# Another order for the first steps of a chunked state-space scan with a squared-ReLU network

## The chip, the cores and the metric

The kernel runs on one core of one Trainium2 chip. The metric is the device time of one launch in microseconds, the median of three runs.

## The reference

Two stages, float32 in and out. Batch 4, 8 heads, 768 positions, head dimension D = 32, state dimension N = 16, chunks of 32; the network has 256 inputs and 2048 hidden units.

```python
for c in range(24):                                  # chunks of 32 positions
    cum = cumsum(log(clip(a[c], 1e-6, 1)))
    L = exp(cum[i] - cum[j]) * (i >= j)
    y = ((C @ B.T) * L) @ x + (C @ state) * exp(cum)
    state = exp(sum(la)) * state + sum_j B[j] x[j] exp(cum[-1] - cum[j])
h = relu(y.reshape(3072, 256) @ w_in)                # 256 -> 2048
out = (h * h) @ w_out                                # 2048 -> 256
```

## The kernel before, in words

Work is cut into 12 units (`UNITS`): unit k is one batch and 256 positions, all 8 heads; units 0 to 3 are the first 256 positions of the four batches. In a unit two positions (r = 0, 1) share a partition, and two halves (i or u = 0, 1) of 64 partitions each are carried through. A unit gives 256 rows of y, held transposed in a tile `T`, and these rows then go through the network as block a, b, c and so on, in 8 tiles of 256 hidden units each.

Nothing is scheduled by the compiler's order: `ORDER` is a string, and `one` reads it word by word and records one step for each word, on the engine that the step or the word's suffix names (v VectorE or DVE, a ScalarE or ACT, p GpSimd or POOL, s SyncE or SP). Every engine and every DMA queue runs its own steps in this order, and steps of different engines wait for each other by semaphores. So moving a word moves the step in the queue of its engine, and only there. Loads on SP and ACT share eight completion semaphores in turn; a load waits until the one eight loads ahead of it has landed.

The words that the change and the prediction touch, in the sequence of the work:

- `idn:c`: n matmuls of ones on c columns into a free PSUM bank (L476), which compute nothing that is used and keep TensorE (PE) busy.
- `fa1:a`, `fa0:s` load a for units 0 to 3 in two halves (L115); `la` loads a for the other units (L553, "late a"). `ldC0:l:a` loads heads 0 to 3 of C for unit 0 on ACT's queue, `ldC0:h:s` heads 4 to 7 on SP's, `ldB2:s` all of B for unit 2 (L125).
- `gB2`, `gB3`: a memset of one column of that unit's B tile on POOL (L134). A load of that tile issued later must wait for it, and so must every load behind it on SP.
- `ku`, `ef`, `eb`, `ti`, `pi`, `hd`, `mb`, `pk`, `wm`: constants (identity, causal mask, head selectors; L480, L490, L507, L511, L512) and a first ACT instruction, which loads its table (L487). `jz` zeroes one of the three tiles `jt` (L685).
- `sk`: clip and running product of a (L468, L469); `sp`: its transpose by matmul (L452); `su`, `to`, `fq`, `ps`, `iv`: chunk totals, copies and reciprocals of the running product. `sn1`, `p2`, `pq` are the same for the later units.
- `pc`, `pb`, `px`: C times the running product and B into `jt`, x over the running product into `xs` (L158, L168 or L170, L177). `tr`, `trC`, `trB`: `jt` transposed by PE (L195) and copied by `tc` from PSUM into `bct` (L208, L210). From unit 4 on one DMA transpose on SP does both (L186).
- `mt`: scores of a unit, 16 matmuls (L220). Four masks per unit: `mk` by DVE from PSUM (L229), or `sc` copied out by ACT (L234) and `ms` masked from that copy by POOL or DVE (L238).
- `u`: the unit's contribution to the state (L245); `sf` scales it (L343), `ca` applies the state to C, `in` (or `ina`, `inb` in halves) masked scores times xs (all L245). `t0:aa` copies the two halves of y of unit 0 into `T` on ACT, `t0:av` on ACT and DVE (L208, L210); `us` copies the state out.
- `wi`, `wo`: the four tiles each of w_in and w_out, converted to bf16 by POOL's DMA (L139, L143).
- `a0` to `l7`: first layer of block a to l, hidden tile 0 to 7, with ReLU on ACT (L403, L408); `qa0` and so on: the square on DVE (L414); `A0` to `L7`: second layer (L430), and with tile 7 the output copy and its store on SP (L437, L438).
- `fr` gives one PSUM bank back to the steps that follow.

The change lies in the first seven lines of the string; from `a7 qa5 iv:16:32 px2` on the words are the same.

Of the kernel before, what the change touches and what calls it, by code (L numbers as in the profile page):

```python
# [30 lines left out]
def kernel(  # L31
# [16 lines left out]
    ORDER = """
        id13:128 fa1:a la fa0:s ku ef ldx0:h:a eb id6:128 ti id5:128 gB3 pi ldB0:l:a hd ldC0:l:a ldB0:h:s ldC0:h:s
        ldx0:l:a wm jz0:v mb jz1:v ldB1:s id10:128 sk pbh0:a id11:128 pk pbl0:p wi0 sp pc0:v ldC1:s trB0 wi1 su  # L50
        iv1:0:8 trC0 tcC0:0:v tcB0:2:a id5:128 tcC0:1:a ps pb1:a to px0:v jz2:v mt0 id4:128 u0:67 ldx1:s pc1:p fq
        sc0 mk0 id5:128 mk0 ms0:p tr1 tc1:1:v sc0 tc1:0:a sf0 mt1 ldB2:s wo0 ldC2:s ms0:v ldx2:s id3:128 in0 ca0
        iv:8:16 id7:256 px1:p t0:aa id1:128 mk1 a0 a1 mk1 mk1 mk1 u1 ina1 inb1 sn1 us0 sf1 qa0 a3 ldC3:s wi2 fr p2
        wi3 ca1 qa1 wo1 pc2 pb2:a t1:vv us1 iv:32:64 a2 zb0 qa2 zb1 A0 ldB3:s wo2 ldx3:s b3 qb3 b0 pq b2 b1 tr2
        wo3 sb1 qa3 qb0 A1 b5 b4 qb1 qb2 qb5 tc2:1:v qb4 tc2:0:a a5 B0 b6 B1 a7 qa5 iv:16:32 px2 a6 mt2 B3 A2 sc2
        u2 b7 us2 pb3:a pc3 mk2 qa6 px3 mk2 A5 ms2:v mk2 ld4 qb6 sf2 a4 qa7 B5 pc4 A6 A3 ld5 pb4 ina2 inb2 tr4 ca2
        t2:aa tr3 B4 B2 tc3:0:a tc3:1:a u3:45 qb7 ld6 ld7 mt3 qa4 B6 mk3 mk3 mk3 mk3 us3 c4 c5 c0 A4 A7 B7 c6 qc0
        za3 qc4 c1 qc5 qc6 sa3 px4 qc1 pc5 pb5 bk c2 rg4 tr5 C0 mk4 mk4 qc2 c7 qc7 sb0 c3 qc3 d2 d1 C5 za4 afC2 d0
        C1 px5 C4 qd2 zb3 C6 C3 qd0 d3 C2 mk4 mk4 C7 px6 sa4 rg5 qd3 sb3 pc6 zb4 sb4 pb6 D0 d4 qd1 tr6 mk5 za5 zb5
        sa5 sb5 D1 iv:64:96 mk5 d5 qd4 D2 pb7 d6 qd5 d7 qd6 D3 zb2 e0 qd7 mk5 e1 qe0 sb2 D4 mk5 D5 ld8 pc7 e2 qe1  # L60
        D6 e3 qe2 px7 D7 rg6 e4 qe3 za6 sa6 tr7 zb6 mk6 e5 qe4 sb6 e6 qe5 e7 qe6 mk6 E0 E1 E2 E3 ld9 px8 mk6 f0
        qe7 E4 f1 qf0 pc8 E5 pb8 E6 mk6 f2 qf1 f3 qf2 E7 rg7 mk7 F0 f4 qf3 za7 tr8 F1 F2 f5 qf4 f6 qf5 f7 qf6 g0
        qf7 zb7 sa7 sb7 mk7 F3 mk7 F4 pc9 pb9 px9 ld10 g1 qg0 F5 mk7 g2 qg1 F6 g3 qg2 F7 rg8 za8 zb8 sa8 sb8 g4
        qg3 G0 mk8 tr9 g5 qg4 G1 mk8 g6 qg5 G2 g7 qg6 G3 mk8 h0 qg7 G4 pc10 pb10 px10 ld11 h1 qh0 G5 mk8 h2 qh1 G6
        h3 qh2 G7 rg9 za9 zb9 sa9 sb9 h4 qh3 H0 mk9 tr10 h5 qh4 H1 mk9 h6 qh5 H2 h7 qh6 H3 mk9 i0 qh7 H4 pc11 pb11
        px11 i1 qi0 H5 mk9 i2 qi1 H6 i3 qi2 H7 rg10 za10 zb10 sa10 sb10 i4 qi3 I0 mk10 tr11 i5 qi4 I1 mk10 i6 qi5
        I2 i7 qi6 I3 mk10 j0 qi7 I4 j1 qj0 I5 mk10 j2 qj1 I6 j3 qj2 I7 rg11 za11 zb11 sa11 sb11 j4 qj3 J0 mk11 j5
        qj4 J1 mk11 j6 qj5 J2 j7 qj6 J3 mk11 k0 qj7 J4 k1 qk0 J5 mk11 k2 qk1 J6 k3 qk2 J7 rg12 k4 qk3 K0 k5 qk4 K1
        k6 qk5 K2 k7 qk6 K3 l0 qk7 K4 l1 ql0 K5 l2 ql1 K6 l3 ql2 K7 l4 ql3 L0 l5 ql4 L1 l6 ql5 L2 l7 ql6 L3 ql7"""
# [694 lines left out]
```

## Time and profile before

| | |
|---|---|
| three runs | 117.47, 116.82, 117.33 us; median 117.33 us |
| the profiled execution | span 115.2 us from the first to the last instruction; no other time is given for it |
| PE matmuls | 108.6 us busy, 94% of the span, 1674 instructions |
| DVE, ACT, POOL | 84.4, 76.7, 49.5 us busy |
| DMA | 13.47 MB; the queue of SP takes 44.8% of 16 engines' span, the weights' queue 10.9% |

Busy time is counted from the first to the last instruction, issue of DMAs not included. Matmuls overlap: a row of x4 with 0.60 us follows the next row after 0.44 us. PEld is the weight load of TensorE, "DMA share" the mean busy share of the 16 DMA engines (over 1 where packets of two kinds overlap), and an "issue" in a chain is time in which the engine waited for nothing that the profile shows. "DMA to landing" is from the start of the issuing instruction to the last byte's completion. Times in the rows are from the start of the span.

### The profile page before, as it was taken

The page shows a single profiled execution, that of the slowest core. Times are in us where ns is not written, and L with a number is a line of the kernel's source. Part 1 is how long each engine was busy: PE and PEld are TensorE (multiplying, and loading weights), DVE is VectorE, ACT ScalarE, POOL GpSimd, SP SyncE. Part 2 cuts the span into 40 slices and gives each one's busy share as a digit, 9 for nine tenths or more (in the row PEclk, how much of TensorE's full clock was granted, in tenths as well). Part 3 has the DMA queues.
Part 4 walks back from the last instruction along what each step waited for, and adds up shares of the span by engine and source line. Part 5 has one row for each costly group of instructions (what it writes and reads, how often), then busy time and mean ns, then how long its engine had stood idle before and what let it go on. Part 6 is the DMA issues. An engine that isn't in the chain of part 4 may idle for free.

```text
span 115.2 us, 4100 instructions
## 1 busy us (share of the span) xinstructions
PE 108.6 (94%) x1674; PEld 97.4 (85%) x1674; DVE 84.4 (73%) x187; ACT 76.7 (67%) x161; POOL 49.5 (43%) x102
## 2 busy tenths in 40 slices
PE   7978799999999979999999999999999999999990
PEld 7956589988898959989989989989989899899980
DVE  2469989688699969969965989849668488445530
ACT  0665568966598464787486686786777776876840
POOL 7378972067895675548602669038020020000000
PEclk9999999999999999999999999999999999999998
DMA  0999999999979945908818628442041020020202
GB/s 19 203 179 164 193 212 185 211 192 179 185 133 185 308 73 128 173 1 190 153 41 178 130 93 156 100 126 42 0 136 32 0 94 6 1 90 0 95 1 91
DMA packets 47815, 13.47 MB, mean 117 GB/s; under 512 B 44276, under 2 KB 45876, under 8 KB 47796
## 3 DMA queue, kind: packets, MB, share of 16 engines
q1 hardware_dynamic: 43828, 10.64, 44.8%
q0 software_dynamic: 1664, 2.10, 10.9%
q10 hardware_dynamic: 2304, 0.48, 2.0%
q8 instruction: 13, 0.21, 0.8%
q14 instruction: 6, 0.05, 0.2%
HBM read 10.58 MB, written 3.15 MB: 119 GB/s over the span
## 4 chain that ended last, share of the span: by engine, by line
PE 83%; DMA 7%; DVE 2%; issue 1%; POOL 1%; ACTq 1%; ACT 1%; POOLq 0%
PE pp L403 36%; PE pp L430 34%; PE pp L245 7%; DMA bct<-jt 5%; PE pp L220 4%; DMA B_nat<-in_B_dram 3%; PE pp L476 1%; DVE mts L229 1%; PE pp L195 1%; POOL xs L177 1%; PE pp L452 1%; DVE xs L177 1%; ACTq L125 0%; POOL jt L170 0%; ACTq L115 0%
## 5 line engine op out<-in xcount | busy, mean ns | idle before, releaser
L408 ACT ACTIVATE hb<-pp 128x512 bf16<-128x512 f32 x96 | 55.0, 599 | 26.0 <-PE pp L403 24.4
L430 PE MATMUL pp<-w_out_b,h 128*128 128x256 bf16 (+1 forms) x400 | 54.3, 268 | 0.0
L414 DVE TENSOR_TENSOR h<-hb 128x512 bf16<-128x512 bf16 x96 | 46.0, 497 | 11.2 <-ACT hb L408 10.8
L403 PE MATMUL pp<-T,w_in_b 128*128 128x256 bf16 x384 | 54.2, 273 | 0.0
L403 PEld LDWEIGHTS <-w_in_b 128*128 128x128 bf16 x384 | 41.4, 114 | 2.0 <-issue 1.0
L430 PEld LDWEIGHTS <-h 128*128 128x128 bf16 x400 | 37.6, 98 | 4.3 <-issue 0.8
L229 DVE TENSOR_TENSOR mts<-pp,mask 128x512 bf16<-128x512 f32 x45 | 29.6, 678 | 4.1 <-PE pp L220 4.1
L331 POOL TENSOR_TENSOR Sd<-z,Pquad 128x256 bf16<-128x256 f32 x16 | 11.0, 690 | 32.1 <-DVE z L315 25.9
L177 POOL TENSOR_TENSOR xs<-x_nat,Pinv 128x256 bf16<-128x256 f32 (+1 forms) x19 | 14.5, 777 | 6.5 <-DVE Pinv L546 3.7
L158 POOL TENSOR_TENSOR jt<-C_nat,P_sb 128x128 bf16<-128x128 f32 x22 | 9.6, 453 | 1.9 <-DMA C_nat<-in_C_dram 1.3
L476 PE MATMUL pp<-const-bfloat16-1.0 128*128 128x128 bf16 (+1 forms) x70 | 7.4, 281 | 0.8 <-PEq L748 0.8
L476 PEld LDWEIGHTS <-const-bfloat16-1.0 128*128 128x128 bf16 x70 | 6.4, 129 | 1.3 <-issue 1.2
L315 DVE SCALAR_TENSOR_TENSOR z<-z,Ptot,us 128x64 f32<-128x64 f32 x8 | 2.2, 281 | 6.3 <-ACT us L299 5.4
L245 PE MATMUL pp<-mts,xs 64*32 64x128 bf16 x384 | 6.0, 219 | 0.8 <-issue 0.8
L437 ACT COPY osb<-pp 128x512 f32<-128x512 f32 x11 | 6.3, 583 | 0.4 <-PE pp L430 0.4
L220 PE MATMUL pp<-bct 32*64 32x256 bf16 x192 | 5.1, 279 | 1.4 <-DMA bct<-jt 0.7
L170 POOL CAST jt<-B_nat 128x128 bf16<-128x128 f32 x17 | 5.0, 318 | 1.6 <-DVE a_cl L468 1.6
L245 PEld LDWEIGHTS <-xs 64*32 64x32 bf16 x384 | 4.1, 90 | 1.4 <-issue 1.2
L282 ACT CAST T<-pp 128x512 bf16<-128x512 f32 x7 | 4.1, 592 | 0.4 <-PE pp L245 0.2
L245 PE MATMUL pp<-bct,Sd 128*128 128x128 bf16 x40 | 4.2, 219 | 0.0
L208 ACT CAST T<-pp 128x256 bf16<-128x256 f32 x8 | 2.6, 375 | 2.4 <-PE pp L245 2.3
L220 PEld LDWEIGHTS <-bct 32*64 32x64 bf16 x192 | 2.1, 102 | 2.4 <-DMA bct<-jt 0.8
...
## 6 DMA issues: line engine op xcount, KB each, us to landing
...
B_nat<-in_B_dram SPq DMA_DIRECT2D x11, 128.0 KB, 3.8
C_nat<-in_C_dram SPq DMA_DIRECT2D x11, 128.0 KB, 3.8
...
x_nat<-in_x_dram ACTq DMA_DIRECT2D x2, 128.0 KB, 3.6
bct<-jt SPq DMA_TRANSPOSE x8, 2.8
```

The source lines that it names most:

```text
L158: eng.tensor_tensor(out=_fap(jt[k % 3], 128 + 144 * g, [[384, 2], [32, 4], [1, 16]]), in0=_fap(loaded[k]["C"], 128 * g, [[16, 2], [32, 4], ...
L177: eng.tensor_tensor(out=_fap(xs, 256 * r, [[256, 2 // n], [32, 8], [1, 32]]), in0=_fap(loaded[k]["x"], 32 * r, [[32, 2 // n], [64, 8], [1, ...
L220: nc.tensor.matmul(pp[64 * u:64 * u + 64, q, r * 256:r * 256 + 256], bct[32 * q:32 * q + 32, r, 0, u * 64:u * 64 + 64], _fap(bct[32 * q:32 ...
L229: nc.vector.tensor_tensor(out=live[k]["mts"][:, q].rearrange("p r g i -> p (r g i)"), in0=pp[:, q, :], in1=mask, op=ALU.mult)
L245: nc.tensor.matmul(dst, w, v, start=bool(need), stop=False, skip_group_check=True, **({} if pos is None else {"tile_position": pos}))
L331: nc.gpsimd.tensor_tensor(out=_fap(S_d, 0, [[128, 2], [32, 4], [1, 32]]), in0=_fap(z, 0, [[32, 2], [0, 4], [1, 32]]), in1=_fap(Pquad, 4 * ...
L403: nc.tensor.matmul(pp[:, h, i * 256:(i + 1) * 256], _fap(w, g * w.shape[2] + (o // 2) * 512 + 2 * (o % 2) + i, [[4, 128]]), T[blk][:, g].r ...
L408: nc.scalar.activation(out=hb.rearrange("p i t -> p (i t)"), in_=pp[:, h, :], func=AF.Relu)
L414: nc.vector.tensor_tensor(out=h2, in0=hb, in1=hb, op=ALU.mult)
L430: nc.tensor.matmul(dst, h2[:, i, r * 128:(r + 1) * 128], w_out_b[gi][:, 2 * o + i, c0:c1], start=first, stop=(fp == 7 and i == 1), skip_gr ...
L437: nc.scalar.copy(out=osb, in_=pp[:, 6 if blk == 1 else 7, :])
L476: nc.tensor.matmul(pp[:, h, 0:int(cols)], ones_b[:, 0:128], ones_b[:, 0:int(cols)] if dep is None else dep, start=True, stop=True, skip_gr ...
```

## The change

The first seven lines of `ORDER` are written anew; no function changes. On SP, a, C, B and x of unit 0 come before late a; on ACT the loads of unit 0 come in the order a, C, B, x, the heads of x in one load on each queue. The first w_in tile is issued on POOL ahead of the copy of B of unit 0, and the first w_out tile ahead of the masks. The scan of a is recorded ahead of the causal mask. Idle matmuls are 12 of 512 columns instead of 63 of 128 and 7 of 256. The gate on unit 3's B is gone, and one on unit 2's B stands behind unit 1's C, so that unit 2's loads and all behind them on SP wait for it. Unit 0's masks, state, product and `T` follow each other directly, ahead of the transposes of unit 1; the zeroing of the third `jt` comes after them. The second scan moves behind the first tiles of blocks a and b, whose order changes too.

```diff
     ORDER = """
-        id13:128 fa1:a la fa0:s ku ef ldx0:h:a eb id6:128 ti id5:128 gB3 pi ldB0:l:a hd ldC0:l:a ldB0:h:s ldC0:h:s
-        ldx0:l:a wm jz0:v mb jz1:v ldB1:s id10:128 sk pbh0:a id11:128 pk pbl0:p wi0 sp pc0:v ldC1:s trB0 wi1 su
-        iv1:0:8 trC0 tcC0:0:v tcB0:2:a id5:128 tcC0:1:a ps pb1:a to px0:v jz2:v mt0 id4:128 u0:67 ldx1:s pc1:p fq
-        sc0 mk0 id5:128 mk0 ms0:p tr1 tc1:1:v sc0 tc1:0:a sf0 mt1 ldB2:s wo0 ldC2:s ms0:v ldx2:s id3:128 in0 ca0
-        iv:8:16 id7:256 px1:p t0:aa id1:128 mk1 a0 a1 mk1 mk1 mk1 u1 ina1 inb1 sn1 us0 sf1 qa0 a3 ldC3:s wi2 fr p2
-        wi3 ca1 qa1 wo1 pc2 pb2:a t1:vv us1 iv:32:64 a2 zb0 qa2 zb1 A0 ldB3:s wo2 ldx3:s b3 qb3 b0 pq b2 b1 tr2
-        wo3 sb1 qa3 qb0 A1 b5 b4 qb1 qb2 qb5 tc2:1:v qb4 tc2:0:a a5 B0 b6 B1 a7 qa5 iv:16:32 px2 a6 mt2 B3 A2 sc2
+        id3:512 fa1:a fa0:s ef jz0:v ldC0:l:a ldC0:h:s eb id2:512 ldB0:l:a ldB0:h:s hd ti ldx0:l:a ldx0:h:s la ku pi
+        id1:512 sk wm mb jz1:v wi0 ldB1:s ldC1:s sp id1:512 pk id1:512 pc0:v iv1:0:8 trC0 su pbh0:a pbl0:p tcC0:0:v
+        tcC0:1:a trB0 wi1 tcB0:2:a id1:512 px0:v ps to mt0 fr id1:512 u0:67 ldx1:s wo0 fq sc0 mk0 id1:512 mk0 sc0
+        ms0:p sf0 ms0:v pb1:a pc1:p ca0 in0 t0:av jz2:v iv:8:16 tr1 tc1:1:v tc1:0:a id1:512 a0 mt1 gB2 ldB2:s ldC2:s
+        ldx2:s px1:p a1 wi2 wi3 mk1 mk1 mk1 mk1 u1 ina1 inb1 sf1 ca1 wo1 pc2 pb2:a us0 t1:va us1 a2 a3 qa0 qa1 zb0
+        zb1 b0 b1 qa2 qa3 ldC3:s wo2 ldB3:s ldx3:s b2 qb0 qb1 b3 A0 A1 qb2 qb3 wo3 B0 B1 sn1 tr2 sb1 b5 b4 qb5
+        tc2:1:v qb4 tc2:0:a p2 pq iv:32:64 a5 b6 a7 qa5 iv:16:32 px2 a6 mt2 B3 A2 sc2
...
```

More of the change, by code (lines that the diff above doesn't have):

```diff
@@ L54 @@
-        wi3 ca1 qa1 wo1 pc2 pb2:a t1:vv us1 iv:32:64 a2 zb0 qa2 zb1 A0 ldB3:s wo2 ldx3:s b3 qb3 b0 pq b2 b1 tr2
-        wo3 sb1 qa3 qb0 A1 b5 b4 qb1 qb2 qb5 tc2:1:v qb4 tc2:0:a a5 B0 b6 B1 a7 qa5 iv:16:32 px2 a6 mt2 B3 A2 sc2
-        u2 b7 us2 pb3:a pc3 mk2 qa6 px3 mk2 A5 ms2:v mk2 ld4 qb6 sf2 a4 qa7 B5 pc4 A6 A3 ld5 pb4 ina2 inb2 tr4 ca2
-        t2:aa tr3 B4 B2 tc3:0:a tc3:1:a u3:45 qb7 ld6 ld7 mt3 qa4 B6 mk3 mk3 mk3 mk3 us3 c4 c5 c0 A4 A7 B7 c6 qc0
-        za3 qc4 c1 qc5 qc6 sa3 px4 qc1 pc5 pb5 bk c2 rg4 tr5 C0 mk4 mk4 qc2 c7 qc7 sb0 c3 qc3 d2 d1 C5 za4 afC2 d0
@@ L59 @@
[L59 to L68, printed above, removed]
@@ L69 @@
-        k6 qk5 K2 k7 qk6 K3 l0 qk7 K4 l1 ql0 K5 l2 ql1 K6 l3 ql2 K7 l4 ql3 L0 l5 ql4 L1 l6 ql5 L2 l7 ql6 L3 ql7"""
+        id3:512 fa1:a fa0:s ef jz0:v ldC0:l:a ldC0:h:s eb id2:512 ldB0:l:a ldB0:h:s hd ti ldx0:l:a ldx0:h:s la ku pi
+        id1:512 sk wm mb jz1:v wi0 ldB1:s ldC1:s sp id1:512 pk id1:512 pc0:v iv1:0:8 trC0 su pbh0:a pbl0:p tcC0:0:v
+        tcC0:1:a trB0 wi1 tcB0:2:a id1:512 px0:v ps to mt0 fr id1:512 u0:67 ldx1:s wo0 fq sc0 mk0 id1:512 mk0 sc0
+        ms0:p sf0 ms0:v pb1:a pc1:p ca0 in0 t0:av jz2:v iv:8:16 tr1 tc1:1:v tc1:0:a id1:512 a0 mt1 gB2 ldB2:s ldC2:s
@@ new lines @@
+        ldx2:s px1:p a1 wi2 wi3 mk1 mk1 mk1 mk1 u1 ina1 inb1 sf1 ca1 wo1 pc2 pb2:a us0 t1:va us1 a2 a3 qa0 qa1 zb0
+        zb1 b0 b1 qa2 qa3 ldC3:s wo2 ldB3:s ldx3:s b2 qb0 qb1 b3 A0 A1 qb2 qb3 wo3 B0 B1 sn1 tr2 sb1 b5 b4 qb5
+        tc2:1:v qb4 tc2:0:a p2 pq iv:32:64 a5 b6 a7 qa5 iv:16:32 px2 a6 mt2 B3 A2 sc2 u2 b7 us2 pb3:a pc3 mk2 qa6 px3
+        mk2 A5 ms2:v mk2 ld4 qb6 sf2 a4 qa7 B5 pc4 A6 A3 ld5 pb4 ina2 inb2 tr4 ca2 t2:aa tr3 B4 B2 tc3:0:a tc3:1:a
+        u3:45 qb7 ld6 ld7 mt3 qa4 B6 mk3 mk3 mk3 mk3 us3 c4 c5 c0 A4 A7 B7 c6 qc0 za3 qc4 c1 qc5 qc6 sa3 px4 qc1 pc5
@@ new lines @@
+        pb5 bk c2 rg4 tr5 C0 mk4 mk4 qc2 c7 qc7 sb0 c3 qc3 d2 d1 C5 za4 afC2 d0 C1 px5 C4 qd2 zb3 C6 C3 qd0 d3 C2 mk4
+        mk4 C7 px6 sa4 rg5 qd3 sb3 pc6 zb4 sb4 pb6 D0 d4 qd1 tr6 mk5 za5 zb5 sa5 sb5 D1 iv:64:96 mk5 d5 qd4 D2 pb7 d6
+        qd5 d7 qd6 D3 zb2 e0 qd7 mk5 e1 qe0 sb2 D4 mk5 D5 ld8 pc7 e2 qe1 D6 e3 qe2 px7 D7 rg6 e4 qe3 za6 sa6 tr7 zb6
+        mk6 e5 qe4 sb6 e6 qe5 e7 qe6 mk6 E0 E1 E2 E3 ld9 px8 mk6 f0 qe7 E4 f1 qf0 pc8 E5 pb8 E6 mk6 f2 qf1 f3 qf2 E7
+        rg7 mk7 F0 f4 qf3 za7 tr8 F1 F2 f5 qf4 f6 qf5 f7 qf6 g0 qf7 zb7 sa7 sb7 mk7 F3 mk7 F4 pc9 pb9 px9 ld10 g1 qg0
@@ new lines @@
+        F5 mk7 g2 qg1 F6 g3 qg2 F7 rg8 za8 zb8 sa8 sb8 g4 qg3 G0 mk8 tr9 g5 qg4 G1 mk8 g6 qg5 G2 g7 qg6 G3 mk8 h0 qg7
+        G4 pc10 pb10 px10 ld11 h1 qh0 G5 mk8 h2 qh1 G6 h3 qh2 G7 rg9 za9 zb9 sa9 sb9 h4 qh3 H0 mk9 tr10 h5 qh4 H1 mk9
+        h6 qh5 H2 h7 qh6 H3 mk9 i0 qh7 H4 pc11 pb11 px11 i1 qi0 H5 mk9 i2 qi1 H6 i3 qi2 H7 rg10 za10 zb10 sa10 sb10
+        i4 qi3 I0 mk10 tr11 i5 qi4 I1 mk10 i6 qi5 I2 i7 qi6 I3 mk10 j0 qi7 I4 j1 qj0 I5 mk10 j2 qj1 I6 j3 qj2 I7 rg11
+        za11 zb11 sa11 sb11 j4 qj3 J0 mk11 j5 qj4 J1 mk11 j6 qj5 J2 j7 qj6 J3 mk11 k0 qj7 J4 k1 qk0 J5 mk11 k2 qk1 J6
@@ L70 @@
+        k3 qk2 J7 rg12 k4 qk3 K0 k5 qk4 K1 k6 qk5 K2 k7 qk6 K3 l0 qk7 K4 l1 ql0 K5 l2 ql1 K6 l3 ql2 K7 l4 ql3 L0 l5
+        ql4 L1 l6 ql5 L2 l7 ql6 L3 ql7"""
     WIN = [(0, 2), (2, 4), (4, 6), (6, 8)]
```

## The prediction

> **What bounds the kernel now.** I read the page first, then the stretches by time, then the chain of waits, then the timeline of the first 17 us engine by engine, and last the DMA.
>
> ```profile
> span 115.2 us, 4100 instructions
> PE 108.6 (94%) x1674; PEld 97.4 (85%) x1674; DVE 84.4 (73%) x187; ACT 76.7 (67%) x161; POOL 49.5 (43%) x102
> ```
>
> The span is 115.2 us; the median of the three runs, 117.33 us, has 2.1 us around it. The sums below are made in the span, and what they give is taken off 117.33. TensorE (PE) is the bound on average. The stretches, whose columns are length, busy time by engine, clock, DMA share and GB/s, say where it isn't:
>
> ```profile
> 14.45:42.10 27.65, 27.64 (x449) 24.19 (x448) 24.21 (x52) 20.09 (x46) 16.77 (x32) 1.00 1.06 189
> 7.00:8.00 1.00, 0.83 (x19) 0.73 (x19) 0.79 (x3) 0.46 (x3) 0.43 (x1) 1.00 0.68 141
> 10.00:11.00 1.00, 0.81 (x44) 0.61 (x51) 1.00 (x5) 0.00 (x0) 0.81 (x2) 1.00 0.84 134
> 16.00:24.00 8.00, 8.00 (x91) 7.37 (x89) 6.39 (x18) 7.33 (x18) 2.65 (x5) 1.00 1.21 199
> ```
>
> From 14.45 to 42.10 PE is full. The chain of waits (start, length, what) names one wait ahead of that and one behind it:
>
> ```profile
> 13.64 0.80 issue
> 37.51 5.21 DMA bct<-jt
> ```
>
> The timeline has the second wait's end, with the idle time before it in brackets:
>
> ```profile
> 42.76 0.42 PE L220 MATMUL pp<-bct 32*64 32x256 bf16 x16 [0.67 <-DMA bct<-jt]
> ```
>
> So there are two regimes. Before 14.45 the order of small steps sets when PE becomes full. At 42.76 unit 5's scores (L220) wait for a DMA transpose of jt. After that nothing in the trace holds PE up. A gain of g in the front therefore reaches the end only if that transpose comes earlier too: the scores start at the later of (42.09 - g) and (42.72 - d), with d what the transpose gains.
>
> **The front, step by step.** Rows of the timeline are start, length, engine, line, operation and count; the landing row belongs to the two loads above it.
>
> ```profile
> 0.80 0.39 ACTq L115 DMA_DIRECT2D a_nat<-in_a_dram  x1
> 1.61 0.42 SPq L115 DMA_DIRECT2D a_nat<-in_a_dram  x1
> DMA to landing us min/median/max: 1.7/2.4/3.2
> 4.91 0.22 DVE L468 TENSOR_SCALAR a_cl<-a_nat 64x128 f32<-64x128 f32 x1 [1.23 <-DMA a_nat<-in_a_dram]
> 5.16 0.42 DVE L469 TENSOR_TENSOR_SCAN cp<-a_cl,const-float32-0.0 64x128 f32<-64x128 f32 x1
> 0.85 4.75 PE L476 MATMUL pp<-const-bfloat16-1.0 128*128 128x128 bf16 x45 [0.85 <-PEq L748]
> 5.72 0.43 PE L452 MATMUL pp<-eye_f,cp 64*64 64x32 f32 x8
> 6.19 0.49 DVE L158 TENSOR_TENSOR jt<-C_nat,pp 128x128 bf16<-128x128 f32 x2 [0.61 <-PE pp L452]
> 7.97 0.42 PE L220 MATMUL pp<-bct 32*64 32x256 bf16 x16 [0.17 <-ACT bct L208]
> ```
>
> *Loads.* SP's half of a is issued at 1.61, behind late a, and takes 3.2 us to 4.8; ACT's half, first on its queue, takes 1.7. With both first, both land near 0.81 + 1.7 = 2.5. The scan starts at 2.6 in place of 4.91 and, by its own 0.67 us, ends at 3.3. The idle matmuls ahead of L452 are 6 of 512 columns instead of 45 of 128; at 4.75/45 = 0.106 us per 128 columns they take 2.53 us, to 3.4. L452 starts at 3.45 (before: 5.72), C is there (issued second, near 1.24; the 1.7 to 3.2 us of the a row put it at 2.9 to 4.4, and I take 3.8), and L158 follows at 4.05.
>
> *Scores of unit 0.* Two idle matmuls (0.85 us) hold the transposes until 4.9; then transposes, ACT's and DVE's copies and one more idle matmul, which took 1.78 us from L158 to L220 in the rows above, take 2.25 here, since those idle matmuls end 0.4 after L158: scores at 6.3, 1.65 earlier. ACT issues four loads where before had five, so its table load and copies come no later. Late a moves behind x on SP; its one reader, the second scan, moves behind the first tiles, so that costs nothing.
>
> ```profile
> 8.65 1.22 DVE L229 TENSOR_TENSOR mts<-pp,mask 128x512 bf16<-128x512 f32 x2
> 9.11 1.14 POOL L238 TENSOR_TENSOR mts<-sc,mask 128x512 bf16<-128x512 bf16 x1
> 10.38 0.41 DVE L238 TENSOR_TENSOR mts<-sc,mask 128x512 bf16<-128x512 bf16 x1
> 10.82 0.44 PE L245 MATMUL pp<-mts,xs 64*32 64x128 bf16 x32
> 11.31 0.65 ACT L208 CAST T<-pp 128x256 bf16<-128x256 f32 x2 [1.32 <-PE pp L245]
> 10.19 0.42 PE L220 MATMUL pp<-bct 32*64 32x256 bf16 x16 [0.54 <-DVE bct L210]
> 10.88 2.42 DVE L229 TENSOR_TENSOR mts<-pp,mask 128x512 bf16<-128x512 f32 x4
> 14.45 0.32 PE L245 MATMUL pp<-mts,xs 64*32 64x128 bf16 x9 [0.80 <-issue]
> 14.78 0.42 DVE L343 TENSOR_TENSOR Sd<-pp,Pquad 128x256 bf16<-128x256 f32 x1 [0.52 <-PE pp L245]
> ```
>
> *Masks, state, copies of unit 0.* DVE does two masks from 6.8 (1.22), the state (0.41) and the copied mask (0.41): 8.7. The memset of jt2 and unit 1's copy no longer stand between. POOL's mask runs 7.5 to 8.6. L245 starts at 8.75 (before: 10.82). T is copied half by DVE, half by ACT: 9.2 to 9.6 instead of 11.31 to 11.96. That is 2.3 us won for T.
>
> *Unit 1 gives most of it back.* POOL now does the copied mask before C of unit 1, so jt is ready at 9.4, the transposes run 9.45 to 9.95, and DVE, which has T (0.4), the jt2 memset (0.38) and a reciprocal (0.24) in front of its bct copy, ends that at 10.4. Unit 1's scores start at 10.45, where before had 10.19. The four masks (2.42 us) end at 13.4, before 13.3. Two first-layer tiles, which before ran while the masks were made, mostly lie in front of them now, so PE has nothing else: the second half of L245 ends at 13.8, the state (L343 waits for the end of L245 in the row above, so here too) at 14.2, and from the carry at 14.4 PE is full. In before the same point, with the second scan's matmuls set aside, is 14.77 + 0.12 of carry = 14.89. So g = 14.89 - 14.4 = 0.5 us, not 2.3. Either side of it: the a row's 3.2 us in place of 1.7 leaves g = -1.0; a transfer as fast as I took, with the 0.85 of idle matmuls hidden behind C, gives 1.3.
>
> *The stall at 13.64.* It lies inside one row of equal matmuls whose masks were done at 13.30, so it is not data. [...] If the stall only moves, 0.80 comes off g: -0.3.
> [...]
>
> *Weights.* The first w_in tile is issued ahead of the B copy and the picks' end, at about 3.5.
>
> ```profile
> 5.80 1.63 POOL L139 DMA_DIRECT2D w_in_b<-in_moe_w_in_dram  x2
> DMA to landing us min/median/max: 5.0/6.2/7.4
> ```
>
> 5.0 to 6.2 us puts it at 8.5 to 9.7; its first reader stands at 10.1. The B copy behind it on POOL waits 0.8 us for it and still ends at 4.9. At nothing, then, and 0.5 if 7.4 holds.
>
> *Loads held back.* Unit 2's B is issued behind a memset on POOL at 9.4 instead of at 6.33, and C2, x2 and all of SP's later loads queue behind that wait.
>
> ```profile
> 6.33 0.79 SPq L125 DMA_DIRECT2D B_nat<-in_B_dram  x1
> DMA to landing us min/median/max: 6.4/6.4/6.4
> DMA to landing us min/median/max: 7.5/7.5/7.5
> B_nat<-in_B_dram SPq DMA_DIRECT2D x11, 128.0 KB, 3.8
> ```
>
> The landings are B2's, C2's and the median of all B. ACT's copy of B2 stands in front of its half of T1, so B2 must land by 14.1. By the median it lands at 13.2, by its old 6.4 at 15.9. I take the median: x1 is nearly through by then, and before had C1 and x1 in front of it.
>
> **The second half: d.** Unit 4's C bounds POOL, and from there SP issues without rest:
>
> ```profile
> 27.80 0.94 POOL L158 TENSOR_TENSOR jt<-C_nat,P_sb 128x128 bf16<-128x128 f32 x2 [0.51 <-DMA C_nat<-in_C_dram]
> 29.24 1.32 SPq L186 DMA_TRANSPOSE bct<-jt  x1
> 36.29 1.04 SPq L438 DMA_DIRECT2D out_dram<-osb  x2
> ```
>
> Transpose of unit 4, six loads, two stores, transpose of unit 5 at 37.51: all shift with C4, on which POOL waited, and C4 comes when the DMA has moved all before it. That work is the same. The engines were at 1.21 when loaded from both sides and at 0.68 and 0.84 in two stretches; unit 1's loads and three weight tiles now stand ready there. That is worth up to (0.53 + 0.37)/1.21 = 0.75; holding unit 2 back may lose 0.2 near 13. Ends: 0 (SP's issues decide alone) and 0.9; below 0 only by the late loads of the third rival. I take d = 0.65, nearer to the 0.75 of the two stretches.
>
> Sum: the scores of unit 5 start at the later of 42.09 - 0.5 = 41.59 and 42.72 - 0.65 = 42.07, so 42.07 (0.04 more for the issue) against 42.76: **0.65 us off, 116.7 us**. Any g between 0.0 and 1.3 gives the same.
>
> **Rivals.**
>
> *The front's gain carries through.* If C4 gains 1.7 us and more, PE's side decides: g = 1.3 plus the 0.67 of the wait, 1.7 to 2.0 off: 115.5. Against: the DMA share of 1.06 over 27.65 us leaves no such room.
>
> *Nothing moves (the transpose of unit 5 stays).* d = 0 and g above -0.6: 117.3. For: SP's six loads and two stores back to back. Against: they start behind C4.
>
> *Slower: held-back loads come too late.* B2 takes its old 6.4 us from 9.45: 15.85, then its copies (0.5), us (0.27) and T (0.4): T1 at 17.0 instead of 15.3, so 1.7 lost and g = -1.2. C2, issued near 10, takes 7.5: POOL is stuck until 17.5, and the third w_out tile, which is issued behind it at 18.3 instead of 15.42, lands by its old 8.0 us at 26.3.
>
> ```profile
> DMA to landing us min/median/max: 8.0/8.0/8.0
> 24.96 0.60 PE L430 MATMUL pp<-w_out_b,h 128*128 128x256 bf16 x4
> ```
>
> Its reader stands at 24.96 + 1.2 = 26.2; the fourth tile, 0.6 later, adds some 0.7. PE reaches unit 5 at 42.09 + 1.9 = 44.0: 1.2 slower, **118.6 us**. It decides from a B2 that lands after 14.8. For: the landings of before under weights. Against: by the end of unit 1's loads little of SP is in front of it.
>
> *Slower: a cold TensorE.* The 45 matmuls run at 0.106 us per 128 columns; later ones take half of that:
>
> ```profile
> 19.40 1.47 PE L403 MATMUL pp<-T,w_in_b 128*128 128x256 bf16 x12
> ```
>
> With the row of four above, (1.47 - 0.60)/8 = 0.109 us for 256. Before kept PE busy from 0.85 to 5.6 without a gap; now idle matmuls of 2.5 us, then small ones with gaps wait on a, C and B. If full speed comes only after the first tiles, the PE steps on the path (L452, L220 twice, L245 twice, 0.42 on the mean by the rows above, 2.1 us) take up to twice as long: g = 0.5 - 2.1 = -1.6, PE is there at 43.7, and 118.3.
> [...]
>
> **How the numbers follow.** What a measurement of this kernel can tell from no change is 0.5%, 0.59 us. Forecast (0.1 to 1.1 off) 0.50, of which 0.32 over 0.59; gain carried through 0.10; nothing moves 0.12 (0.08 within, 0.04 slower); held-back loads late 0.20; cold 0.08 (0.02 within). Faster 0.32 + 0.10 = 0.42; same 0.18 + 0.08 + 0.02 = 0.28; slower 0.04 + 0.20 + 0.06 = 0.30. The range goes from the carried gain, 115.5, to the late loads, 118.6; the forecast's own range is 116.2 to 117.2.
>
> **What would show it.** Right: L452 near 3.5 in the timeline, unit 0's scores near 6.3, T near 9.2; unit 1's four masks still ending near 13.4; PE full from 14.4; no 0.80 stall; the transpose of unit 5 issued near 36.9 and its scores near 42.1. Wrong: ACT idle before B2's copy past 14.1, PE waiting on L430 near 25, idle matmuls past 6 us still at 0.42 us per 512 columns, or unit 5's scores without a wait.

## The result, and the profile after

The changed kernel takes 120.80 us (median of four executions, 120.37 to 121.47); the kernel before, run beside it, 117.40. The ratio is 1.033, with an interval of 1.028 to 1.037: 3.4 us slower, where 0.65 us off was forecast.

Ratios here and below leave out executions over 1.5% above the fastest of the same kernel; where many executions of a kernel lie there, the median, which is over all of them, says something else, and both are given.

The page of the changed kernel:

```profile
span 118.7 us, 3985 instructions
PE 111.5 (94%) x1616; PEld 94.1 (79%) x1616; DVE 84.8 (71%) x187; ACT 77.2 (65%) x161; POOL 49.6 (42%) x102
```

PE is busy for 2.9 us more with 58 fewer matmuls: some of them ran slower. The timeline, in the columns of the prediction, step by step to where PE becomes full:

```profile
3.49 0.64 PE L452 MATMUL pp<-eye_f,cp 64*64 64x32 f32 x8
4.06 1.04 PE L476 MATMUL pp<-const-bfloat16-1.0 128*128 128x512 bf16 x2
4.18 0.48 DVE L158 TENSOR_TENSOR jt<-C_nat,pp 128x128 bf16<-128x128 f32 x2 [0.24 <-PE pp L452]
6.84 0.65 PE L220 MATMUL pp<-bct 32*64 32x256 bf16 x16
7.64 1.29 DVE L229 TENSOR_TENSOR mts<-pp,mask 128x512 bf16<-128x512 f32 x2 [0.87 <-PE pp L220]
9.64 0.66 PE L245 MATMUL pp<-mts,xs 64*32 64x128 bf16 x32
10.06 0.76 POOL L158 TENSOR_TENSOR jt<-C_nat,P_sb 128x128 bf16<-128x128 f32 x2 [0.70 <-DMA C_nat<-in_C_dram]
10.31 0.37 ACT L208 CAST T<-pp 128x256 bf16<-128x256 f32 x1 [0.43 <-PE pp L245]
11.71 1.06 PE L403 MATMUL pp<-T,w_in_b 128*128 128x256 bf16 x4
12.70 0.49 PE L220 MATMUL pp<-bct 32*64 32x256 bf16 x16
13.25 2.48 DVE L229 TENSOR_TENSOR mts<-pp,mask 128x512 bf16<-128x512 f32 x4 [1.37 <-PE pp L220]
14.79 1.05 POOL L177 TENSOR_TENSOR xs<-x_nat,Pinv 128x512 bf16<-128x512 f32 x1 [3.93 <-DMA x_nat<-in_x_dram]
15.89 0.25 PE L245 MATMUL pp<-xs,jt 64*32 64x64 bf16 x16 [2.14 <-POOL xs L177]
17.07 0.40 PE L245 MATMUL pp<-bct,Sd 128*128 128x128 bf16 x2 [0.47 <-DVE Sd L343]
17.26 3.99 PE L403 MATMUL pp<-T,w_in_b 128*128 128x256 bf16 x24
46.24 0.42 PE L220 MATMUL pp<-bct 32*64 32x256 bf16 x16
```

The reader is to see three things. L452 comes at 3.49 as forecast, and everything behind it comes later than forecast: unit 0's scores 0.5 us, T 1.1, unit 1's scores 2.25. Then PE waits 2.14 us for x of unit 1. Then a row of 24 matmuls of 256 columns takes 3.99 us, where the prediction's rate (0.60 us for a row of four, 0.109 for each further one) makes 2.78. Unit 5's scores at 46.24 wait for nothing, so PE's side has lost 46.24 - 42.09 = 4.15 us; before waited 0.67 us there, which leaves 3.48, the 3.5 of the two spans.

The landings of unit 1's x, first after and then before:

```profile
L125 SPq DMA_DIRECT2D x_nat<-in_x_dram x1: 1649/1649/1649, 4.7 to 4.7; - x1
DMA to landing us min/median/max: 9.9/9.9/9.9
...
L125 SPq DMA_DIRECT2D x_nat<-in_x_dram x1: 903/903/903, 5.4 to 5.4; - x1
DMA to landing us min/median/max: 5.7/5.7/5.7
```

It is issued 0.7 us earlier and lands at 14.6 instead of 11.1. C of unit 1 lands at 9.9 (POOL starts on it at 10.06) instead of 7.9. The stretches (length, busy time by engine, clock, DMA share, GB/s):

```profile
10.00:12.00 2.00, 1.93 (x33) 1.04 (x15) 1.27 (x4) 0.85 (x2) 0.80 (x3) 1.00 1.19 207
14.00:16.00 2.00, 0.11 (x20) 0.19 (x24) 1.73 (x3) 1.04 (x4) 1.21 (x2) 1.00 0.46 93
16.00:18.00 2.00, 1.53 (x54) 1.10 (x47) 1.41 (x5) 0.50 (x2) 2.00 (x4) 0.58 1.30 213
18.00:20.00 2.00, 2.00 (x13) 1.49 (x12) 1.66 (x5) 1.26 (x4) 1.98 (x5) 0.57 1.06 169
```

From 10 to 12 the DMA engines are full, and by the trace's packets the weights' queue takes a share of 0.85 in the first microsecond and 1.05 in the second, SP's loads 0.34 and 0.13; before had 0.29 and 0.85 for the weights against 0.55 and 0.24. At 14 to 16 they are half empty: x of unit 1 has landed at 14.6, and unit 2's B, issued at 10.9 behind its gate, lands at 15.3. The clock is at half from 16.3 to 19.7. It was so ahead of 12.9 too, where the profile has no record of it and shows 1.00: the row of two idle matmuls at 4.06 (1.04 us, 0.61 for such a row in e14) and that of four tiles at 11.71 (1.06 us, 0.60 at full clock) tell.

### The profile page after: what moved, and what is told of

Same layout as the page of the kernel before. It is cut to its first block, busy times and chain, and to the rows that moved or that the text cites. A ratio compares the mean times of both kernels' runs of the same rounds, so it can differ in the third digit from the quotient of the medians.

```text
span 118.7 us, 3985 instructions
## 1 busy us (share of the span) xinstructions
PE 111.5 (94%) x1616; PEld 94.1 (79%) x1616; DVE 84.8 (71%) x187; ACT 77.2 (65%) x161; POOL 49.6 (42%) x102
## 3 DMA queue, kind: packets, MB, share of 16 engines
q0 software_dynamic: 1664, 2.10, 10.9%
## 4 chain that ended last, share of the span: by engine, by line
PE 79%; DMA 8%; DVE 3%; SPq 3%; ACT 1%; issue 1%; POOL 1%; ACTq 0%; POOLq 0%
PE pp L403 35%; PE pp L430 34%; DMA x_nat<-in_x_dram 8%; PE pp L245 7%; PE pp L220 3%; SPq L125 2%; DVE mts L229 1%; POOL xs L177 1%; ACT hb L408 1%; DVE mts L238 1%; DVE Sd L343 1%; DVE h L414 1%; SPq L553 1%; PE pp L195 1%; SPq L115 0%
## 5 line engine op out<-in xcount | busy, mean ns | idle before, releaser
L403 PE MATMUL pp<-T,w_in_b 128*128 128x256 bf16 x384 | 55.6, 279 | 0.0
L414 DVE TENSOR_TENSOR h<-hb 128x512 bf16<-128x512 bf16 x96 | 44.8, 483 | 12.5 <-ACT hb L408 11.9
L403 PEld LDWEIGHTS <-w_in_b 128*128 128x128 bf16 x384 | 42.1, 116 | 3.3 <-issue 1.5
L331 POOL TENSOR_TENSOR Sd<-z,Pquad 128x256 bf16<-128x256 f32 x16 | 11.1, 694 | 31.3 <-DVE z L315 25.7
L177 POOL TENSOR_TENSOR xs<-x_nat,Pinv 128x256 bf16<-128x256 f32 (+1 forms) x19 | 14.4, 777 | 5.0 <-DMA x_nat<-in_x_dram 3.9
L476 PE MATMUL pp<-const-bfloat16-1.0 128*128 128x512 bf16 x12 | 6.2, 623 | 0.8 <-PEq L748 0.8
L220 PE MATMUL pp<-bct 32*64 32x256 bf16 x192 | 5.7, 294 | 0.1
L245 PE MATMUL pp<-xs,jt 64*32 64x64 bf16 x160 | 3.0, 199 | 2.1 <-POOL xs L177 2.1
L245 PEld LDWEIGHTS <-jt 64*32 64x32 bf16 x160 | 1.7, 90 | 4.0 <-issue 2.5
L245 PEld LDWEIGHTS <-Sd 128*128 128x128 bf16 x40 | 3.0, 99 | 2.0 <-DVE Sd L343 1.7
```

Of the source, the lines that this page charges most:

```text
L177: eng.tensor_tensor(out=_fap(xs, 256 * r, [[256, 2 // n], [32, 8], [1, 32]]), in0=_fap(loaded[k]["x"], 32 * r, [[32, 2 // n], [64, 8], [1, ...
L220: nc.tensor.matmul(pp[64 * u:64 * u + 64, q, r * 256:r * 256 + 256], bct[32 * q:32 * q + 32, r, 0, u * 64:u * 64 + 64], _fap(bct[32 * q:32 ...
L245: nc.tensor.matmul(dst, w, v, start=bool(need), stop=False, skip_group_check=True, **({} if pos is None else {"tile_position": pos}))
L331: nc.gpsimd.tensor_tensor(out=_fap(S_d, 0, [[128, 2], [32, 4], [1, 32]]), in0=_fap(z, 0, [[32, 2], [0, 4], [1, 32]]), in1=_fap(Pquad, 4 * ...
L403: nc.tensor.matmul(pp[:, h, i * 256:(i + 1) * 256], _fap(w, g * w.shape[2] + (o // 2) * 512 + 2 * (o % 2) + i, [[4, 128]]), T[blk][:, g].r ...
L414: nc.vector.tensor_tensor(out=h2, in0=hb, in1=hb, op=ALU.mult)
```

## The experiments

Each kernel is the changed kernel or the one before with a few words of the string moved. "Before" is the median of the kernel before, run beside them, "ratio" the ratio to it with its interval.

| run | what | median us | before | ratio |
|---|---|---|---|---|
| e1 | changed, first w_out tile late | 121.00 | 117.66 | 1.026 (1.018 to 1.034) |
| e2 | changed, no gate | 122.03 | 117.66 | 1.041 (1.033 to 1.049) |
| e3 | changed, long idle block | 120.28 | 117.66 | 1.023 (1.018 to 1.029) |
| e4 | before, thin idle block | 118.22 | 117.66 | 1.004 (0.999 to 1.009) |
| e5 | e1 and e3 together | 120.39 | 117.89 | 1.024 (1.008 to 1.040) |
| e6 | e5, first w_in tile late too | 119.70 | 117.89 | 1.019 (1.004 to 1.034) |
| e7 | before, both tiles early | 120.28 | 117.89 | 1.029 (1.016 to 1.041) |
| e8 | before, new loads, fewer idle | 117.75 | 117.89 | 0.996 (0.989 to 1.003) |
| e9 | changed, both tiles late | 120.05 | 117.33 | 1.022 (1.016 to 1.027) |
| e10 | e9, no gate | 120.06 | 117.33 | 1.012 (1.006 to 1.017) |
| e11 | e8, more idle | 117.40 | 117.33 | 0.998 (0.994 to 1.003) |
| e12 | before, gate on unit 2's B, not 3's | 119.37 | 117.33 | 1.008 (1.003 to 1.013) |
| e13 | e10, long idle block | 120.11 | 117.64 | 1.011 (1.002 to 1.021) |
| e14 | e13, waits filled | 118.22 | 117.64 | 1.011 (1.007 to 1.015) |
| e15 | before, three parts put in | 120.56 | 117.64 | 1.028 (1.022 to 1.034) |
| e16 | before, new loads alone | 116.99 | 117.64 | 0.996 (0.992 to 1.000) |
| e17 | before, idle matmuls merged | 116.46 | 117.83 | 0.993 (0.988 to 0.997) |
| e18 | e16 and e17 | 116.53 | 117.83 | 0.993 (0.989 to 0.997) |

### One part of the changed kernel undone, or put into the kernel before: e1 to e4

```diff
# e1: the first w_out tile behind the gate
-  u0:67 ldx1:s wo0 fq ... mt1 gB2 ldB2:s
+  u0:67 ldx1:s fq ... mt1 gB2 wo0 ldB2:s
# e2
-  mt1 gB2 ldB2:s
+  mt1 ldB2:s
# e3
-  id3:512 fa1:a
+  id8:512 fa1:a
# e4, on the kernel before: 14 idle matmuls instead of 45 ahead of L452
-  id13:128 ... id6:128 ti id5:128 ... id10:128 sk pbh0:a id11:128
+  id4:128 ... id2:128 ti id2:128 ... id3:128 sk pbh0:a id3:128
```

> The changed kernel with one word moved: the first w_out tile is issued behind the gate memset (near 10.9 us) and not at 6.5. Theory A (the early weight tiles hold up unit 1's x on the DMA): x1 lands near 11.5 to 12.5 instead of 14.65, POOL's product of x1 no longer waits 3.9 us, PE's 2.14 us wait for xs is gone or under 0.4, and the time is 117.3 to 118.5 us. Theory B (the cold TensorE is the main loss): the clock still opens near 12.9, and the time stays over 119.5. Theory C (the gate on unit 2's B is the main loss): within 0.6 of 120.8.

> The changed kernel without the gate on unit 2's B: unit 2's loads are issued right behind unit 1's x. Theory C (the gate): B2's copy on ACT no longer waits, and the time falls by 1 us or more, to 119.8 or less. Theory A (early weights): x1 still lands at 14 or later, PE still waits 2 us for xs, and the time is 120.2 to 121.5. Theory B (cold TensorE): no change either.

> The changed kernel with eight idle matmuls of 512 columns at the start instead of three: TensorE is busy without a gap from 0.85 to 5.5, about as in the kernel before, and L452 comes 2.1 us later. Theory B (cold TensorE): the clock opens by 6, the steps from there on take half, and the time falls to 119.8 or less. Theory A (early weights): x1 still lands at 14 to 15, and PE waits for it; the front's work is done with time to spare, so the time stays at 120.2 to 121.5.

> The kernel before with 14 idle matmuls of 128 columns instead of 45 ahead of L452, so that TensorE is idle for about 3 us there and its clock opens later. Theory B: the steps on the path up to 14 us take up to twice as long, 2 us or more in all: 119.4 or more. Theory A: the clock is worth under 1 us, 117.4 to 118.4, since the loads come at their old times.

From the timelines of e1 (first two rows) and e3 (whose last row stops after 22 of the 24):

```profile
12.71 1.04 POOL L176 TENSOR_TENSOR xs<-x_nat,Pinv 128x512 bf16<-128x512 f32 x1 [0.83 <-DMA x_nat<-in_x_dram]
17.69 5.33 PE L402 MATMUL pp<-T,w_in_b 128*128 128x256 bf16 x24
...
15.72 0.25 PE L244 MATMUL pp<-xs,jt 64*32 64x64 bf16 x16 [2.16 <-POOL xs L176]
17.04 4.16 PE L402 MATMUL pp<-T,w_in_b 128*128 128x256 bf16 x22
```

In e1, x1 lands 2.1 us earlier and the 2.14 us wait is gone, as theory A said, and the time hardly moves (ratio 1.026 against 1.033). Two limits stood close behind. DVE's masks ended at 13.25 + 2.48 = 15.73 in the changed kernel, 0.16 before PE began. And in e1's profile, which is of its longest execution (122.12 us), the clock stays at half: the same 24 matmuls take 5.33 us, and the row of four behind them, at 22.81, takes 0.66. In e3 unit 1's scores, at 12.58, take 0.42 us, full speed as theory B said; PE then waits 2.16 us for x1, and behind that wait 22 of the 24 matmuls take 4.16 us, half speed again for a part of them. e2, above all of its ranges, says that the gate is not the loss here (x1 lands at 14.2 without it), e4 that a thin idle block alone costs the kernel before about 0.5 us, which is not clear of noise. So none of theories A, B and C is the whole cause.

### Two parts undone, and the weights alone: e5 to e8

```diff
# e6 (e5 is e1's and e3's edits; e6 adds this)
-  jz1:v wi0 ldB1:s ... pbl0:p tcC0:0:v
+  jz1:v ldB1:s ... pbl0:p wi0 tcC0:0:v
# e7, on the kernel before
-  jz1:v ldB1:s ... pbl0:p wi0 sp ... ldx1:s pc1:p ... ldB2:s wo0 ldC2:s
+  jz1:v wi0 ldB1:s ... pbl0:p sp ... ldx1:s wo0 pc1:p ... ldB2:s ldC2:s
# e8, on the kernel before
-  fa1:a la fa0:s ku ef ldx0:h:a eb ... ldB0:l:a hd ldC0:l:a ldB0:h:s ldC0:h:s ldx0:l:a wm
-  ... id10:128 sk pbh0:a id11:128 pk
+  fa1:a fa0:s ku ef ldC0:l:a ldC0:h:s eb ... ldB0:l:a hd ldB0:h:s ldx0:l:a ldx0:h:s la wm
+  ... sk pbh0:a pk
```

> The changed kernel with both edits of the runs that moved little by themselves: eight idle matmuls of 512 columns at the start, and the first w_out tile behind the gate. Theory D (the late x of unit 1 and the cold TensorE are two limits side by side: taking one away leaves the other): x1 lands near 12.6, the wait for xs is under 0.6 us, the clock stays open through unit 1, and the time is 116.8 to 118.3 us, 2.5 us or more under the changed kernel. Theory A (weights alone) and theory B (clock alone) both leave it at 119.5 or more, since each of them has failed alone.

> As the run before, and the first w_in tile also back behind the copy of B of unit 0 (issued near 5.6 instead of 3.55). If packets of weights hold up unit 1's loads one by one, B1 lands near 8, C1 near 8.5 and x1 near 11 (before: 11.08), and the time is 0.3 to 1.0 us below the run with w_out alone: 116.2 to 117.5. If w_in's place doesn't matter, within 0.4 of it.

> The kernel before with only the places of the first w_in and the first w_out tile as in the changed kernel (issued near 3.7 and 7.5 instead of 5.8 and 10.2). Theory A and D: x1 lands at 13 or later instead of 11.08, PE waits 1 us or more for xs of unit 1, the clock closes in some executions, and the time is 118.5 to 120.5. If the weights are harmless: within 0.6 of 117.5.

> The kernel before with only the order of the first loads of the changed kernel (a, C, B, x, late a) and 24 instead of 45 idle matmuls of 128 columns ahead of L452, so that L452 comes near 3.5. The prediction's reading (an earlier front is worth up to 1.2 us, then unit 5's transpose holds): 116.2 to 117.2. Theory D: the short idle block leaves TensorE cold, and what the front gains is lost to steps at half speed: 117.3 to 119.5, with the clock opening after 8 us.

e7 settles most. Its loads of unit 1 (C, then x) and what they hold, from the landings and the timeline:

```profile
L124 SPq DMA_DIRECT2D C_nat<-in_C_dram x1: 532/532/532, 4.8 to 4.8; - x1
DMA to landing us min/median/max: 6.4/6.4/6.4
L124 SPq DMA_DIRECT2D x_nat<-in_x_dram x1: 3076/3076/3076, 5.4 to 5.4; - x1
DMA to landing us min/median/max: 9.3/9.3/9.3
11.28 0.76 POOL L157 TENSOR_TENSOR jt<-C_nat,P_sb 128x128 bf16<-128x128 f32 x2 [4.42 <-DMA C_nat<-in_C_dram]
13.02 0.60 PE L219 MATMUL pp<-bct 32*64 32x256 bf16 x16 [0.52 <-DVE bct L209]
```

Two early weight tiles and nothing else put C1 at 11.1 (7.9 before) and x1 at 14.6 (11.1), POOL stands 4.42 us for C, with unit 0's copied mask queued behind it, and unit 1's scores come 2.8 us late. It costs 2.4 us by the median and 3.3 by the ratio. All twenty profiles agree on C1: it takes 5.6 to 7.6 us from issue to landing in the seven with an early first w_in tile (5.8 in the changed kernel, 6.3 in e1, 6.4 in e7), and 2.9 to 4.2 in the other thirteen (2.9 in before, 3.3 in e16, 4.2 in e9). e5 came out where theories A and B had it and not where D had, and e6 missed both of its ranges: with both tiles back and a long idle block the changed kernel is still 1.8 us over (2.2 by the ratio), so theory D's two limits were not all. e8 shows that the new load order with a shorter idle block loses nothing and wins nothing sure.

### What is left without the weights: e9 to e12

e9 has e1's and e6's moves of the two tiles, e10 drops the gate too, e11 is e8 with 31 idle matmuls ahead of L452 and 5 behind it.

```diff
# e12, on the kernel before
-  id5:128 gB3 pi ... sf0 mt1 ldB2:s wo0
+  id5:128 pi ... sf0 mt1 gB2 ldB2:s wo0
```

> The changed kernel with the first w_in tile and the first w_out tile back in their places behind the copy of B and behind the gate, and nothing else undone: this is the changed kernel without its early weights. Theory E (the early weights are nearly all of the loss; the rest of the change is worth about nothing): C of unit 1 lands near 7.6, x near 11.4, and the time is within 0.8 of the kernel before. Theory D (weights and cold clock, two limits): TensorE stays at half speed past 9 us and the time is 1 to 2.5 us over the kernel before, 118.5 to 120.

> As the run before, without the gate on unit 2's B. If the gate makes unit 2's loads late for their use (C theory), 0.4 us or more faster than with it, and B2 lands before 14.5 us; if holding them back is harmless, within 0.4; if unit 2's loads take DMA time from unit 1's x and the weights, up to 1 us slower, as it was with the early weights.

> The kernel before with the changed order of the first loads, 31 idle matmuls of 128 columns ahead of L452 and 5 behind it in the place of the 45. In the run with 24, PE stood idle 0.78 and 0.51 us around L452 and the clock closed from 7.3 to 14.2. If the clock is what keeps the earlier front from its gain, it stays open here in most executions and the time is 115.8 to 116.8, 0.6 or more under the kernel before; if the second half holds the time (unit 5's transpose), 117.0 to 117.8.

> The kernel before with the gate on unit 2's B (issued behind a memset near 10.3 instead of at 6.3) in place of the one on unit 3's B, and nothing else. The prediction's rival of held-back loads: B2 lands at 15 or later, ACT's copy of it holds T1, and the time rises by 0.6 to 1.5 us, to 118 to 119. Its forecast of a 3.8 us landing: B2 near 14.1, C1's and x1's loads through earlier, and the time within 0.5 of the kernel before.

e9 refutes theory E: without its early weights the changed kernel is still 2.7 us over before (2.5 by the ratio), not 3.4. In its profile x1 lands at 13.1 all the same and PE waits 2.50 us for it, with unit 1's scores ahead of that at full speed (0.42 us at 10.86), so theory D's clock at half past 9 us is not there either. e11 came out in its second range. e12's rows (C of unit 2, POOL, PE):

```profile
L124 SPq DMA_DIRECT2D C_nat<-in_C_dram x1: 1723/1723/1723, 10.8 to 10.8; - x1
DMA to landing us min/median/max: 9.1/9.1/9.1
19.92 0.76 POOL L157 TENSOR_TENSOR jt<-C_nat,P_sb 128x128 bf16<-128x128 f32 x2 [5.77 <-DMA C_nat<-in_C_dram]
20.37 0.76 PE L194 MATMUL pp<-eye_b,jt 128*128 128x128 bf16 x5 [2.27 <-POOL jt L157]
```

The gate moved from unit 3's B to unit 2's costs the kernel before 0.9 us by the ratio and 2.0 by the median. B2 lands at 15.8. C2, issued at 10.8 among the weights, takes 9.1 us, and PE waits 2.27 for what POOL makes of it. This is the mechanism of the prediction's slower rival, which also had POOL stuck on C2, though it had PE wait for a w_out tile behind that and not for C2's own product. e10's executions fall in two groups, 117.9 (two) and 119.5 to 120.5 (ten); its timeline has PE idle 1.32 us for the state and 0.79 for the masks, with nothing to fill it. By the median e10 equals e9, by the ratio it is 1% below.

### The clock, and the parts put together: e13 to e16

e13 is e10 with `id8:512` at the start. e14 adds the line below. e15 is e4's, e7's and e12's edits in one, e16 e8's without the cut of idle matmuls.

```diff
# e14
-  pc1:p ca0 in0 ... mk1 mk1 mk1 mk1 u1
+  pc1:p id4:512 ca0 id2:512 in0 ... mk1 mk1 mk1 mk1 id1:512 u1 id1:512
```

> The changed kernel with the early weight tiles, the gate and the thin idle block all taken back; the new order of loads, masks, state, product and tiles stays. Theory F (three limits side by side make the whole loss): within 0.8 of the kernel before, 116.7 to 118.2. Theory G (the new order of unit 0 and of the first tiles costs by itself, since PE now waits 1.3 us for the state and 0.8 us for the masks with nothing to do): 118.4 to 120.

> As the run before, with eight more idle matmuls of 512 columns in the waits of the new order (four ahead of the state's use, two ahead of unit 0's product, one on either side of unit 1's first step). Theory G by way of the clock: no gap of over 0.6 us ahead of unit 1, full clock from about 6 us on, and 0.6 to 1.5 us faster than the run before. If the order costs by its waits themselves, within 0.5 of it; if the filling delays the path, up to 1 us slower.

> The kernel before with the three parts put in and nothing else: early first w_in and w_out tile, the gate on unit 2's B in place of unit 3's, 14 idle matmuls instead of 45 ahead of L452. Theory F: x of unit 1 lands at 14 or later, and the time is that of the changed kernel, 120.2 to 121.8. Theory G: the parts overlap and stay at the cost of the early weights alone, 119.5 to 120.3, or less.

> The kernel before with only the order of the first loads changed and all 45 idle matmuls kept, so that L452 stays near 5.7 and the clock as it was. The steps behind it no longer wait for C and B; if the front is bound by the transfers of unit 1 and of the weights, which come no earlier, the time is within 0.5 of the kernel before; if by the chain from L452, 0.3 to 0.8 us faster.

The first matmuls of unit 0's product in e13, e13's stretch from 17 to 20, then the same stretch of e14:

```profile
10.51 0.28 PE L244 MATMUL pp<-bct,Sd 128*128 128x128 bf16 x2 [1.32 <-DVE Sd L342]
17.00:20.00 3.00, 3.00 (x17) 2.14 (x15) 2.36 (x7) 2.19 (x6) 0.94 (x2) 0.50 1.20 163
...
17.00:20.00 3.00, 3.00 (x29) 2.92 (x28) 2.80 (x9) 3.00 (x8) 1.24 (x2) 1.00 1.21 173
```

Both have PE busy for all of the 3 us; with the waits filled it does 29 matmuls and not 17, at clock 1.00 and not 0.50, and the median falls by 1.9 us, with work that computes nothing. The ratios are the same, 1.011, and so are the fastest executions (117.76 and 117.83 us): what changes is how often an execution comes out longer. Of e14's eleven, seven are under 118.7 us, of e13's six, one; these are few to rest on. What e14 is still over the kernel before, 1.2 us by the ratio and 0.6 by the median, is left for the new order with its fillers: its unit 1 scores start at 12.70 as in the changed kernel, 2.5 us behind before, though L452 starts at 5.63, close to the 5.72 of before. e15 reaches 120.56, the time of the changed kernel, with none of the new order. So theory F holds one way only: the three parts are enough for the loss, but not needed for a good part of it, since with all three back the new order and its idle PE lose 2.5 us at the median (1.3 by the ratio). Two limits of this reading: by the ratio the early tiles alone cost as much as all three (e7 1.029, e15 1.028), and e15's thin idle block is that of e4, where PE stood idle for 3.29 us ahead of L452; the changed kernel has no such wait.

### The stall at 13.64 and unit 5: e17 and e18

```diff
# e17, on the kernel before; e18 has it on top of e16
-  id13:128 ... id6:128 ti id5:128 ... id10:128 sk pbh0:a id11:128
+  id3:512 id1:128 ... id1:512 id2:128 ti id1:512 id1:128 ... id2:512 id2:128 sk pbh0:a id2:512 id3:128
```

> The kernel before with the 45 idle matmuls of 128 columns ahead of L452 replaced by 9 of 512 and 9 of 128: the same idle time, 27 matmuls and 27 weight loads fewer ahead of everything else, nothing else changed. If the 0.80 us stall hangs on the count of instructions, it is gone from its place (L245, behind 39 of 48) and shows elsewhere or nowhere; if it hangs on the step or the time, it stays near 13.6. By the prediction's formula its end is worth only 0.04 us, as unit 5's scores then wait 1.4 us for their transpose: within 0.5 of the kernel before. If the front alone sets the end, 0.6 to 0.8 faster.

> The kernel before with the changed order of the first loads and the merged idle matmuls: the parts of the change that have cost nothing, without early weights, gate and the new order of unit 0. If the transfers of unit 1 and the weights and unit 5's transpose hold the time, 116.6 to 117.4, within 0.6 of the kernel before; if the stall and the front's waits were the bound, 115.8 to 116.5.

The row of e16, which has as many idle matmuls as before, then the same products of unit 1 in e12, then e17's rows (these products again, unit 5's transpose, its scores), then e18's:

```profile
13.76 0.32 PE L244 MATMUL pp<-mts,xs 64*32 64x128 bf16 x9 [0.81 <-issue]
...
13.24 0.57 PE L244 MATMUL pp<-mts,xs 64*32 64x128 bf16 x32
...
13.05 0.57 PE L245 MATMUL pp<-mts,xs 64*32 64x128 bf16 x32
37.49 1.26 SPq L186 DMA_TRANSPOSE bct<-jt  x1
41.48 0.42 PE L220 MATMUL pp<-bct 32*64 32x256 bf16 x16
...
14.93 0.63 PE L403 MATMUL pp<-T,w_in_b 128*128 128x256 bf16 x4 [1.73 <-DMA w_in_b<-in_moe_w_in_dram]
24.41 1.04 POOL L177 TENSOR_TENSOR xs<-x_nat,Pinv 128x512 bf16<-128x512 f32 x1 [5.29 <-DMA x_nat<-in_x_dram]
```

In e16 the stall stays, 0.81 us ahead of the last 9 of the same row of matmuls; with 27 pairs of matmul and weight load fewer (e17), at the same idle time, it is gone and shows nowhere else. But the count is not all: e12's PE has the same matmuls in the same order as before, and all 32 run through in 0.57 us. e17's ratio is 0.993 (0.988 to 0.997): 0.9 us faster than the kernel before, from edits that compute nothing, where 0.6 to 0.8 was the most expected. And its unit 5 scores start at 41.48 without a wait, though their transpose is issued at 37.49, as in before (37.51): in this profile the transfer itself was quicker. In e18 the earlier front meets the second w_in tile (1.73 us) and x of unit 2 (5.29 us), and the load order adds nothing to e17.

## Why the prediction was wrong, step by step

- **The weights: this step failed.** "At nothing, then, and 0.5 if 7.4 holds" weighed the first w_in tile by its own landing and by POOL's wait for the issue. It left out what its packets do to unit 1's C and x, which are issued behind it (6.4 and 9.3 us from issue to landing in e7, 2.9 and 5.7 in before), and it did not cost the first w_out tile at all. e7 measures the term: 2.4 to 3.3 us alone. Taken out of the changed kernel it gives back less, 0.7 us by the medians and 1.3 by the ratios (e9), as other limits stand beside it. The prediction took two single microseconds of the kernel before, with shares of 0.68 and 0.84, for room. Its longer stretches show none:

```profile
3.00:6.00 3.00, 2.87 (x35) 2.73 (x32) 1.29 (x4) 2.08 (x5) 1.11 (x5) 1.00 1.09 202
6.00:9.00 3.00, 2.38 (x57) 1.75 (x55) 2.24 (x7) 1.92 (x9) 2.31 (x5) 1.00 1.00 184
9.00:12.00 3.00, 2.46 (x71) 1.90 (x70) 3.00 (x8) 1.63 (x5) 2.58 (x4) 1.00 1.05 163
```

  In the changed kernel the weights' queue and SP's loads move in the same microsecond, with shares of 0.85 and 0.34 from 10 to 11 us.
- **x of unit 1.** "x1 is nearly through by then" carried the landing of B2. x1 landed at 14.6, and PE's 2.14 us wait for it is on the chain of the changed kernel. B2 landed at 15.3, past the 14.8 from which that rival decided; yet ACT's half of T1 waited 1.53 us for PE, long after its copy of B2, so the rival's condition held and its path did not. e12 shows that path through C2, at 0.9 to 2.0 us.
- **The front.** The loads came as forecast (L452 at 3.49 against 3.45). The steps behind it were priced at full clock. At half clock the scores take 0.65 us, not 0.42, the tile ahead of unit 1's scores 1.06, not 0.60. This was the cold rival, with a chance of 0.08 and a time of 118.3; its slow steps are seen in the changed kernel, and e3, with the longer idle block, has unit 1's scores at 0.42 us. Its worth is 1.9 us by the medians of e13 and e14 and nothing by their ratios. It is not there in each profile: in e10's, whose first idle matmuls are the same, unit 0's scores, at 6.19, take 0.42 us. The prediction looked at the start of the clock only: behind the wait for x1 it is at half again, from 16.3 to 19.7, which makes the 24 matmuls 1.2 us longer (3.99 against 2.78). It also cut 63 small idle matmuls to 12 larger ones without asking which waits they had filled: 1.32 and 0.79 us of them stand open in e10.
- **Unit 1.** "The four masks end at 13.4" was 15.7: C1 2 us late, transposes and a tile at half clock. So g, forecast at +0.5, is -4.15. Of the 4.65 between them, 17.07 - 14.4 = 2.7 lie ahead of the carry, 1.2 in the 24 slow matmuls, and 0.8 I can't place: PE stands idle for only 0.2 us between 17 and 46.24.
- **The stall: gone as forecast, its cause open.** The 0.5 of g counts it as gone. It is gone in the changed kernel, where the 32 matmuls take 0.65 us, and in e17, where they take 0.57. That it hangs on the count of PE instructions is not shown: e16 keeps it at the same matmul, 0.7 us earlier, which speaks for the count, and e12 has it nowhere at an equal count, which speaks against the count alone. What makes the 0.80 us, no run here shows.
- **Unit 5's transpose: wrong.** The formula let a gain of the front count only if SP issues this transpose earlier by d. In e17's profile the front's gain came through with the transpose issued at the same time, as it took 4.0 us at most and not 5.2. The later of the two terms was itself a transfer whose time changes from run to run, not a fixed length.

What stays open: which words of the new order cost its 0.6 to 1.2 us, and why the gate costs the kernel before while taking it out of the changed one does not help: that gave a ratio of 1.041 (e2) against the 1.033 of the changed kernel.
